# q and k in planes of every fourth token, and DMA transposes from pair 4 on, in an attention and feed-forward kernel

## The chip, the cores and the metric

The kernel runs on one core of one Trainium2 chip. The metric is the time of one execution on the device in microseconds (us), the median of several. Executions of one kernel lie within 1.3% of each other here (the kernel before: 345.49 to 350.08 us). A profile is of one execution and has a span of its own, a little shorter than the time (346.3 us). Engines in the profile: PE is TensorE (matmuls), DVE VectorE, ACT ScalarE, POOL GpSimd, SP SyncE; on this kernel SP issues all DMA transfers, in order.

## The reference

Attention over 8 batches and 8 heads, 576 tokens of 64 features each, followed by a feed-forward layer on all 4608 tokens:

```
q_d, k_d, v_d = mean of 4 neighbouring tokens of q, k, v        # 144 tokens
out_d     = softmax(q_d k_d^T / 8) v_d, each row repeated 4 times
out_local = softmax(q k^T / 8, only where |i - j| < 4) v
x         = (out_d + out_local), heads side by side             # 4608 x 512
h         = x @ w_in                                            # 512 x 2048
result    = (h - tanh(h)) @ w_out                               # 4608 x 512
```

## The kernel before

Two heads are one *pair*; there are 32 pairs, four to a batch. For each pair q and k are loaded, cast to bf16 rows (`qr`), transposed so that features lie on partitions (the way *forward*), multiplied (`local` scores in five bands, `pooled` scores on sums of four tokens), exponentiated, masked, multiplied by v, normalised (`ln`), and transposed again (the way *back*) into `x`, which the code calls `xT`.

The feed-forward part runs on TensorE in 9 *dense blocks* of 512 tokens: 64 matmuls for the first product (mm1), 64 for the second (mm2). Block 0 needs batch 0 (pairs 0 to 3). **Block 1 needs pairs 0 to 7**, because tokens 512 to 1023 reach into batch 1; block 2 needs pair 11, block 3 pair 15, and so on.

The order of all this is fixed when the kernel is built. Each operation is registered with an engine, an estimated duration and the data that it reads and writes; a list scheduler with those estimates (*the planner*) then fixes each engine's order. On the chip every engine goes through its list in order and waits where something is not ready. Dense matmuls have the lowest priority, so they fill what attention leaves free.

```python
# cut: loads, casts of the weights, pooled v
        if p >= T_DMA:                      # T_DMA = 16: forward by DMA from pair 16 on
            op("SP", 700, lambda: nc.sync.dma_start_transpose(
                out=qT[s].rearrange("p i a g -> p (i a) g"),
                in_=qr[s].rearrange("p i a c -> p (i a c)")), ...)
            op("DMA", 1300, None, ...)      # the planner's estimate of the transfer
            for i in range(2):              # then a reorder of q and of k
                op("ACT", 600, lambda i=i: A.copy(...), ...)
        else:                               # TensorE: 6 transposes each for q and k
            for i in range(2):
                op("PE", 260 * cold, tr, reads=[("qr", s, i), "ident"], ...)
                op("ACT", 540, lambda i=i, b16=b16: A.copy(...), ...)
# cut: two additions for the sums of four; then, before pair 16,
# local scores (s1) and last-band-and-pooled scores (s2) are two blocks in bank pair "ts"
            op("PE", 420 * cold, s1, reads=qks, writes=ts, pri=pri)
# cut: exp on ACT, mask on DVE
            op("PE", 380 * cold, s2, reads=qks + [("qkd", s)], writes=ts, pri=pri)
# cut: exp, mask, outputs (PE, bank pair "ox"), reciprocal and ln (DVE, from "ox")
        if p >= X_DMA:                      # X_DMA = 16: back by DMA from pair 16 on
            op("SP", 600, lambda: nc.sync.dma_start_transpose(
                out=lT[s], in_=ln[s].rearrange("p n c -> p (n c)")), ...)
            # cut: join on DVE or POOL writes xT
        else:                               # 7 transposes on TensorE, then join on DVE
            op("PE", 370 * cold, back, reads=[("ln", s)], writes=ox, pri=pri)
# dense: pri=5000
            op("PE", 432, lambda part=part: mm(part),
               reads=[...] + [("x", b, j) for b in bs for j in range(NP)],
               writes=[("hy", slot)], pri=5000)
    M2_FIRST, T_DMA, X_DMA, NEW = 16, 16, 16, 16
```

The softmax here doesn't subtract the row's maximum and nothing guards it: scores larger than these inputs give would overflow.

## Time and profile before

| | before |
|---|---|
| time, median of 4 | 347.8 us |
| span of the profile | 346.3 us |
| first dense matmul | 32.1 us |
| x of pair 7 written | 74.9 us |
| block 1 starts | 76.4 us |
| from there to the end | 269.9 us |

The start of a block is read from the timeline: its first mm1 matmul, after the 64 of the block before it. Parts of the page, with each digit of a row standing for a fortieth of the span (9 is 90% busy or more; PEclk is the granted TensorE clock in tenths):

```profile
span 346.3 us, 6847 instructions
PE 328.0 (95%) x2556; PEld 163.5 (47%) x2556; DVE 223.8 (65%) x362; ACT 224.8 (65%) x382; POOL 169.9 (49%) x210
...
PE   6787989999999999999999999899999999999995
...
PEclk9698999999999999999999999999999999999999
DMA  8999999999999998999999999645231000100021
...
PE 69%; DVE 10%; ACT 9%; issue 3%; DMA 3%; POOL 2%; SPq 1%; ACTq 0%; POOLq 0%; DVEq 0%
```

Now the path of pair 4 and the end of pair 7 in the timeline (start, duration, engine, line, operation, out<-in; in brackets the idle time before it and what ended it):

```profile
33.38 0.82 POOL L416 CAST qr_86<-qkn_71 96x768 bf16<-96x768 f32 x1 [1.12 <-DMA qkn_71<-in_k_dram]
36.15 0.42 PE L442 MATMUL ps_ts<-ident,qr_86 96*128 96x96 bf16 x6
...
39.17 0.39 PE L478 MATMUL ps_ts<-qk_88 64*128 64x120 bf16 x8
...
51.55 1.09 DVE L556 TENSOR_TENSOR ln_106<-ps_ox,r_104 128x896 bf16<-128x896 f32 x1
...
71.80 1.09 DVE L556 TENSOR_TENSOR ln_107<-ps_ox,r_105 128x896 bf16<-128x896 f32 x1
...
74.15 0.74 DVE L599 TENSOR_TENSOR xT_68<-ps_ox,od_109 128x576 bf16<-128x576 bf16 x1
76.41 0.39 PE L619 MATMUL ps_hy_538<-xT_65,w_in_sb 128*128 128x512 bf16 x1
```

Pair 7's `ln` ends at 72.9 us and its x is complete 2.0 us later. Block 1 starts 1.5 us after that. So x of pair 7 arrives just in time, with nothing to spare.

### The profile page before, as it was taken

The numbers are of one execution on the slowest core, as the hardware profiler recorded it, in microseconds if no ns is written. First come the engines' busy times: TensorE is split into PE (matmuls) and PEld (weight loads), VectorE is DVE, ScalarE is ACT, GpSimd is POOL, SyncE is SP. The second block draws the span as 40 slices with busy tenths as digits, with TensorE's granted clock in tenths as the row PEclk, the third lists the DMA queues.
The fourth block names the chain that finished last, engine by engine and source line by source line (L and its number), as shares of the span: only waits on it lengthen the run. The fifth ranks groups of instructions, "written<-read, shape, count | busy, mean of one in ns | idle before, by whom it ended". The sixth has DMA issues, their size and how long they took to land.

```text
span 346.3 us, 6847 instructions
## 1 busy us (share of the span) xinstructions
PE 328.0 (95%) x2556; PEld 163.5 (47%) x2556; DVE 223.8 (65%) x362; ACT 224.8 (65%) x382; POOL 169.9 (49%) x210
## 2 busy tenths in 40 slices
PE   6787989999999999999999999899999999999995
PEld 2353445555555554445444444444454444444442
DVE  5675788558897968778867677679774443343300
ACT  4585886768978768787878778599753434343411
POOL 6553555575467856887777786958500000000000
PEclk9698999999999999999999999999999999999999
DMA  8999999999999998999999999645231000100021
GB/s 192 234 374 300 277 262 263 217 216 287 212 222 234 252 234 174 226 231 235 261 221 207 260 233 246 157 92 93 57 85 60 31 32 30 61 32 31 30 93 61
DMA packets 103407, 60.74 MB, mean 175 GB/s; under 512 B 77774, under 2 KB 94670, under 8 KB 103374
## 3 DMA queue, kind: packets, MB, share of 16 engines
q1 hardware_dynamic: 103374, 60.30, 78.5%
q8 instruction: 20, 0.33, 0.4%
q14 instruction: 13, 0.11, 0.1%
HBM read 42.46 MB, written 9.44 MB: 150 GB/s over the span
## 4 chain that ended last, share of the span: by engine, by line
PE 69%; DVE 10%; ACT 9%; issue 3%; DMA 3%; POOL 2%; SPq 1%; ACTq 0%; POOLq 0%; DVEq 0%
PE ps_hy_540 L646 8%; PE ps_hy_538 L619 8%; PE ps_hy_539 L619 7%; PE ps_hy_541 L646 7%; PE ps_hy_538 L646 7%; PE ps_hy_539 L646 6%; PE ps_hy_540 L619 6%; PE ps_hy_541 L619 6%; PE ps_ox L538 3%; DVE qr_87 L416 2%; PE ps_ts L478 2%; DMA qkn_73<-in_k_dram 2%; PE ps_ox L545 2%; PE ps_ts L442 2%; PE ps_ox L389 2%
## 5 line engine op out<-in xcount | busy, mean ns | idle before, releaser
L619 PEld LDWEIGHTS <-w_in_sb 128*128 128x128 bf16 x576 | 53.3, 98 | 62.1 <-issue 3.9
L646 PEld LDWEIGHTS <-gT_110 128*128 128x128 bf16 x320 | 30.2, 98 | 34.5
L646 PEld LDWEIGHTS <-gT_111 128*128 128x128 bf16 x256 | 24.0, 98 | 27.4
L459 POOL TENSOR_TENSOR half<-qk_88 128x576 f32<-128x576 bf16 x14 | 16.4, 1169 | 25.3 <-ACT qk_88 L448 11.2
L459 POOL TENSOR_TENSOR half<-qk_89 128x576 f32<-128x576 bf16 x16 | 18.7, 1167 | 19.8 <-ACT qk_89 L448 12.2
L646 PE MATMUL ps_hy_539<-w_out_sb,gT_110 128*128 128x512 bf16 x80 | 20.7, 379 | 0.0
L646 PE MATMUL ps_hy_540<-w_out_sb,gT_110 128*128 128x512 bf16 x80 | 20.4, 379 | 0.0
L646 PE MATMUL ps_hy_538<-w_out_sb,gT_110 128*128 128x512 bf16 x80 | 20.4, 379 | 0.0
L646 PE MATMUL ps_hy_541<-w_out_sb,gT_110 128*128 128x512 bf16 x80 | 20.1, 379 | 0.0
L432 ACT COPY qk_89<-qT_91 128x576 bf16<-128x576 bf16 x16 | 18.7, 1193 | 0.0
L432 ACT COPY qk_88<-qT_90 128x576 bf16<-128x576 bf16 x16 | 18.4, 1188 | 0.0
L511 ACT ACTIVATE E_100<-ps_ts 128x960 bf16<-128x960 f32 x16 | 15.6, 977 | 3.8 <-PE ps_ts L478 3.8
L556 DVE TENSOR_TENSOR ln_106<-ps_ox,r_104 128x896 bf16<-128x896 f32 x16 | 17.4, 1090 | 0.5
L646 PE MATMUL ps_hy_540<-w_out_sb,gT_111 128*128 128x512 bf16 x64 | 16.9, 379 | 0.0
L646 PE MATMUL ps_hy_541<-w_out_sb,gT_111 128*128 128x512 bf16 x64 | 16.8, 379 | 0.0
L646 PE MATMUL ps_hy_539<-w_out_sb,gT_111 128*128 128x512 bf16 x64 | 16.6, 379 | 0.0
L646 PE MATMUL ps_hy_538<-w_out_sb,gT_111 128*128 128x512 bf16 x64 | 16.4, 379 | 0.0
L511 ACT ACTIVATE E_101<-ps_ts 128x960 bf16<-128x960 f32 x14 | 13.6, 973 | 3.8 <-PE ps_ts L478 3.6
L514 DVE TENSOR_TENSOR E_101<-E_101,mask 128x960 bf16<-128x960 bf16 x16 | 13.1, 820 | 3.9 <-ACT E_101 L511 3.7
L556 DVE TENSOR_TENSOR ln_107<-ps_ox,r_105 128x896 bf16<-128x896 f32 x14 | 15.3, 1090 | 0.4
L514 DVE TENSOR_TENSOR E_100<-E_100,mask 128x960 bf16<-128x960 bf16 x16 | 13.6, 847 | 2.8 <-ACT E_100 L511 2.8
L619 PE MATMUL ps_hy_538<-xT_65,w_in_sb 128*128 128x512 bf16 x36 | 13.9, 385 | 1.2 <-DVE xT_68 L599 1.2
(263 smaller groups left out, 890.1 us busy)
## 6 DMA issues: line engine op xcount, KB each, us to landing
out_dram<-y_115 SPq DMA_DIRECT2D x12, 256.0 KB, 2.6
out_dram<-y_116 SPq DMA_DIRECT2D x12, 256.0 KB, 2.3
out_dram<-y_117 SPq DMA_DIRECT2D x12, 256.0 KB, 3.0
qkn_71<-in_q_dram SPq DMA_DIRECT2D x8, 288.0 KB, 7.8
qkn_71<-in_k_dram SPq DMA_DIRECT2D x8, 288.0 KB, 5.8
qkn_72<-in_q_dram SPq DMA_DIRECT2D x8, 288.0 KB, 5.1
qkn_72<-in_k_dram SPq DMA_DIRECT2D x8, 288.0 KB, 5.5
qkn_73<-in_q_dram SPq DMA_DIRECT2D x8, 288.0 KB, 6.6
```

The source lines that it names most:

```text
L389: T.matmul(pv[:, 0, :], pick[:, t, :], vw[w][:, :, t, 0:64], start=(t == 0), stop=(t == NT - 1))
L416: P.choice([(eng, ns, lambda dst=dst, srt=srt, fn=fn: fn(out=dst, in_=srt)) for eng, ns, fn in REORDER[p >= NEARLY][i]], reads=[("qkn", sn ...
L432: op("ACT", 600, lambda i=i: A.copy(out=full[:, i].rearrange("p (g a) -> p g a", a=A6), in_=qT[s][:, i].rearrange("p a g -> p g a")), read ...
L442: T.transpose(b16[:, G6 * a:G6 * a + G6], qr[s][:, i, a, :], ident[0:G6, 0:G6])
L459: eng.tensor_tensor(out=half, in0=four[:, :, :, 0:2], in1=four[:, :, :, 2:4], op=ALU.add)
L478: T.matmul(sc[:, c:c + NQ[t]], qk[s][rows, k0:k0 + 128], qk[s][rows, QW * t:QW * t + NQ[t]], start=True, stop=True)
L511: op("ACT", 870, lambda: A.activation(out=e1, in_=ps[:, :, 0:480], func=AF.Exp, scale=SCALE), reads=ts, writes=[("E", s, 0)], pri=pri)
L514: op("DVE", 700, lambda: V.tensor_tensor(out=e1, in0=e1, in1=mask[:, 0:480].unsqueeze(1).to_broadcast([128, 2, 480]), op=ALU.mult), reads= ...
L538: T.matmul(po[:, hh, 65 * t:65 * t + 65], E[s][:, c:c + 128], vw[w][:, 2 * jj + hh, t, :], start=True, stop=True)
L556: op("DVE", 1010, lambda: V.tensor_tensor(out=ln[s].rearrange("p n (h d) -> p h n d", d=D), in0=blocks[:, :, :, 0:64], in1=r[s].unsqueeze( ...
L619: T.matmul(ps_hy[slot], w_in_sb[:, dc, fc * 128:(fc + 1) * 128], xT[dc][:, kb * 512:kb * 512 + 512], start=(dc == 0), stop=(dc == N_DC - 1))
L646: T.matmul(ps_hy[slot], gT[g][:, fc, ts * 128:ts * 128 + 128], w_out_sb[:, fc, :], start=(fc == 0), stop=(fc == N_FF - 1))
```

## The change

Its intent: (1) take the transposes of pairs 4 to 15 off TensorE in both directions; (2) load q and k so that a row holds 4 tokens instead of 6, which gives four planes of every fourth token: sums of four become additions of planes, q is used in plane order and only k has to be reordered (`kt`); (3) pack the last band and the pooled scores of pair p with the local scores of pair p+1 into one block of TensorE work, the former now in the outputs' bank pair "ox" for every pair from 4 on. In pairs 0 to 3 the transposes stay on TensorE and the pooled sums become matmuls with the identity. The planner's estimates change with it (one exp from 870 to 970 ns, one mask from 700 to 800, from pair 5 on 300 ns of slack before score blocks and outputs). The core of the diff:

```diff
-    M2_FIRST, T_DMA, X_DMA, NEW = 16, 16, 16, 16
+    M2_FIRST, NEW, LATE = 16, 16, 300
# ... loads: 96 rows of 6 tokens become three chunks of 96 rows of 4 tokens
-    qkn = fixed("qkn", [G6, 2, 2, A6 * D], FP32, NQKN)
-    qT = fixed("qT", [128, 2, A6, G6], BF16, 2)
+    qkn = fixed("qkn", [R, 3, 2, 4 * D], FP32, NQKN)
+    planes = fixed("planes", [128, 4, 2 * G], BF16, NPL)
+    kt = fixed("kt", [128, 608], BF16, 2)
# ... forward: bring_rows(p)
+        if p < NP:                                   # NP = 4
+            return
+        op("SP", 700, lambda: nc.sync.dma_start_transpose(
+            out=planes[pl].rearrange("p a (c g) -> p (a c) g", g=R),
+            in_=qr[s].rearrange("p a c d -> p (a c d)")), ...)
# ... bring_sums(p): k reordered on DVE, ACT or POOL; planes added on DVE or POOL
# ... one score block
+    def scores(p):
+        def mm():
+            mixed_mm(p, flat2(ps_ox), 72 if p >= NEW else 16)
+            if p + 1 < NPAIR:
+                local_mm(p + 1, flat2(ps_ts), range(4), None)
+        keys = mixed_keys(p) + (local_keys(p + 1) if p + 1 < NPAIR else [])
+        op("PE", 640, mm, reads=keys, writes=["ox"] + [("ts", 0), ("ts", 1)], ...)
# ... back: give_back(p)
-        if p >= X_DMA:
+        if p >= NP:
             op("SP", 600, lambda: nc.sync.dma_start_transpose(
                 out=lT[s], in_=ln[s].rearrange("p n c -> p (n c)")), ...)
```

## The prediction

> **What bounds the kernel now.** By the page, PE is busy 95% of a 346.3 us span and holds 69% of the chain of waits. In the timeline a dense matmul (128x512) issues every 0.216 us; 1152 of them make 249 us. The first starts at 32.1 us; attention is interleaved on PE until 254 us.
>
> A second bound hides before 75 us. In the table of 1 us windows the DMA share is at or above 1.0 in every window from 24 to 66 us: w_in, w_out and q, k, v loads queue behind each other (7 to 12 us from issue to landing). Dense block 1 needs pairs 0 to 7. The last x piece of pair 7 is written at about 74.3 us; block 0 runs out of matmuls at 75.4 us. So PE work there is only just enough: removing some gains nothing unless pair 7 is ready earlier.
>
> **What the change removes.** For pairs 4 to 15, 12 forward transposes (0.51 us of PE) and 7 back transposes (0.50 us) per pair: 12.1 us. One score block in place of two saves a switch gap, about 0.13 us per pair, 1.6 us. From pair 16 on, two ACT reorders from SBUF (1.19 us each) become one on any of three engines; ACT and DVE (65% busy each) are off the critical path there. In pairs 0 to 3 the pooled sums move from DVE/POOL (1.17 + 0.74 us on POOL) to 16 short matmuls: 1 to 2 us at most.
>
> **What it adds.** 24 more DMA transposes. In the DMA windows after 225 us, where little else runs, a transpose fills the engines for about 1.35 us (295 KB: 218 GB/s) and lands about 5 us after issue. The Trainium skill, "DMA: Bandwidth & Descriptors", section "Latency and other measured facts", gives 261 GB/s for a transpose with a non-contiguous middle dimension; this trace is somewhat below. The q/k loads get 1 KB rows: about neutral. The score block of pair p also needs pair p+1's k: pair 7 waits for pair 8.
>
> **Cost on the critical path.** The saturated queue gets about five transposes (7 us) before pair 8 lands; each pair's chain gets two landings of 5 to 6 us in place of PE work. I estimate from these durations that pair 7's x arrives at 80 to 88 us instead of 74, while PE runs dry at 67 to 70 us. So pairs 4 to 7's saving is lost and 5 to 14 us more is paid. From there on about 9 us is saved (pairs 8 to 15); later the attention pace (7 to 8 us per pair by DMA) stays under the 8.2 to 8.6 us that PE needs for a pair plus its share of dense work.
>
> Net: between -8 and +6 us. Prediction 344.5 us (334 to 354). Faster by over 2%: 0.36; within 2%: 0.48; slower by over 2%: 0.16.
>
> **What would show it.** Right: PE idle between about 65 and 85 us, ended by x or scores that waited for DMA; block 1 starting after 76 us; from then on about 264 us instead of 270; DMA share at or above 1 until 150 us or later. Wrong: block 1 starting before 75 us (about 335 us); or PE stalls spread over pairs 16 to 31, behind late transposes in a fixed PE order (above 350 us).
>
> **What would make it wrong.** If the queue has slack that I read as saturation, or transposes get in early, the whole 13 us is gained. If SP, which issues all DMAs in order, blocks on transposes, both stages are late.

## More of the kernel before

TensorE is busy throughout and is 69% of the chain of waits. The same by stages, from the table of windows (window; its length; for PE, PEld, DVE, ACT, POOL the busy time and the count of instructions; clock; DMA share; GB/s):

```profile
60.00:80.00 20.00, 19.97 (x214) 11.33 (x212) 12.01 (x21) 13.98 (x26) 13.27 (x16) 1.00 1.20 223
80.00:100.00 20.00, 19.97 (x212) 11.14 (x210) 18.04 (x30) 17.60 (x35) 10.40 (x13) 1.00 1.18 250
160.00:180.00 20.00, 20.00 (x158) 9.78 (x157) 15.09 (x22) 15.62 (x24) 15.30 (x20) 1.00 1.17 231
180.00:200.00 20.00, 20.00 (x162) 10.02 (x161) 14.22 (x24) 15.95 (x26) 15.32 (x18) 1.00 1.14 234
```

Pair 4's k rows are ready at 34.2 us, transposed on TensorE from 36.2 us and scored at 39.2 us.

## The result

| | before | after |
|---|---|---|
| time, median of 4 runs | 347.8 us | 385.8 us |
| span of the profile | 346.3 us | 385.2 us |
| first dense matmul | 32.1 us | 43.3 us |
| x of pair 7 written | 74.9 us | 110.9 us |
| block 1 starts | 76.4 us | 110.4 us |
| from there to the end | 269.9 us | 274.8 us |
| mean granted TensorE clock | 0.984 | 0.929 |

The ratio is 1.109 (95% interval 1.103 to 1.116): the mean time of one kernel's fast runs over that of the other's of the same rounds, so not quite the ratio of the medians above. The change makes the kernel 11% slower. The arithmetic of the spans says where: 34.0 us are lost before block 1 starts, 4.9 us after (34.0 + 4.9 = 38.9 = 385.2 - 346.3). The page after:

```profile
span 385.2 us, 6661 instructions
PE 331.0 (86%) x2396; PEld 165.5 (43%) x2396; DVE 254.6 (66%) x396; ACT 207.4 (54%) x367; POOL 170.8 (44%) x195
...
PE   6866799843479849998899899998999999999996
...
PEclk9998799955569958999999999999999999999999
DMA  8999999999998999999999999996220100101012
...
PE 46%; DVE 13%; DMA 8%; POOL 5%; issue 3%; ACT 1%; SPq 1%; POOLq 0%; ACTq 0%; DVEq 0%
```

and the same stages in the table of windows:

```profile
60.00:80.00 20.00, 15.64 (x109) 7.22 (x107) 11.10 (x15) 9.24 (x17) 9.98 (x11) 0.96 1.14 256
80.00:100.00 20.00, 9.29 (x102) 6.59 (x103) 16.77 (x24) 9.18 (x17) 8.58 (x9) 0.50 1.07 237
160.00:180.00 20.00, 17.98 (x154) 8.88 (x151) 19.57 (x25) 14.59 (x28) 16.60 (x17) 1.00 1.08 222
180.00:200.00 20.00, 18.32 (x167) 9.40 (x166) 19.48 (x26) 15.11 (x29) 19.94 (x20) 1.00 1.15 201
```

Two things stand out. There is a hole in TensorE's row between 76 and 110 us (9.3 of 20 us busy, at half clock). Later, VectorE is nearly full (19.6 of 20 us, 15.1 before) and TensorE isn't (18.0 instead of 20). The path of pair 4, and the end of pair 7, in the timeline after:

```profile
36.65 0.61 POOL L423 CAST qr<-qkn 96x512 bf16<-96x512 f32 x1 [1.14 <-DMA qkn<-in_k_dram]
...
52.06 2.71 SPq L429 DMA_TRANSPOSE planes<-qr  x1
...
61.87 0.39 PE L509 MATMUL ps_ts<-planes,kt 64*128 64x120 bf16 x8
...
70.13 0.65 DVE L442 COPY kt<-planes 128x576 bf16<-128x576 bf16 x1 [5.78 <-DMA planes<-qr]
...
71.48 0.22 PE L509 MATMUL ps_ox<-planes,kt 64*128 64x96 bf16 x2
...
74.75 1.09 DVE L619 TENSOR_TENSOR ln<-ps_ox,r 128x896 bf16<-128x896 f32 x1
...
84.00 1.38 SPq L645 DMA_TRANSPOSE lT<-ln  x1
...
97.02 1.09 DVE L619 TENSOR_TENSOR ln<-ps_ox,r 128x896 bf16<-128x896 f32 x1
...
104.86 1.27 SPq L645 DMA_TRANSPOSE lT<-ln  x1
...
109.49 1.22 DVE L629 TENSOR_TENSOR xT<-lT 128x480 bf16<-128x480 bf16 x1
...
110.39 1.47 PE L687 MATMUL ps_hy<-xT,w_in_sb 128*128 128x512 bf16 x3
110.51 0.42 DVE L635 TENSOR_TENSOR xT<-lT 128x96 bf16<-128x96 bf16 x1
```

The rows of pair 4 were cast by 37.3 us, but SP issued their transpose at 52.1, 14.8 us later, behind loads in its list. Local scores came at 61.9 us instead of 39.2. Pair 4's pooled scores then came only at 71.5, 9.6 us later: they share a block with the local scores of pair 5, and the reorder of pair 5's k (the copy `kt` at 70.1) had waited for pair 5's transpose. The transpose at 84.0 us is pair 4's way back. For pair 7, `ln` ended at 98.1 us, SP issued the transpose at 104.9, and x was complete at 110.9: 12.8 us for a way back that took 2.0. Block 1 starts with it; its fourth matmul still waits for the last piece.

x of pair 7 is 36.0 us late. That is a sum of three differences: pair 4's `ln` 23.2 us later (52.6 to 75.8), three more pairs at 7.4 us each instead of 6.8 (2.0 us), and the longer way back (10.8 us).

### The profile page after: what moved, and what is told of

It is laid out like the page before. It is cut to its first block, busy times and chain, and to the rows that moved or that the text cites. A ratio compares the mean times of both kernels' runs of the same rounds, so it can differ in the third digit from the quotient of the medians.

```text
span 385.2 us, 6661 instructions
## 1 busy us (share of the span) xinstructions
PE 331.0 (86%) x2396; PEld 165.5 (43%) x2396; DVE 254.6 (66%) x396; ACT 207.4 (54%) x367; POOL 170.8 (44%) x195
## 4 chain that ended last, share of the span: by engine, by line
PE 46%; DVE 13%; DMA 8%; POOL 5%; issue 3%; ACT 1%; SPq 1%; POOLq 0%; ACTq 0%; DVEq 0%
PE ps_hy L687 21%; PE ps_hy L714 20%; DVE gT L698 4%; DMA planes<-qr 3%; DMA lT<-ln 2%; DMA vst<-in_v_dram 2%; DVE E L543 2%; PE ps_ox L601 2%; DVE kt L442 1%; DVE ln L619 1%; DVE qkd L453 1%; PE ps_ox L608 1%; POOL kt L442 1%; DVE E L561 1%; POOL half L448 1%
## 5 line engine op out<-in xcount | busy, mean ns | idle before, releaser
L687 PE MATMUL ps_hy<-xT,w_in_sb 128*128 128x512 bf16 x576 | 145.1, 388 | 4.7 <-DVE xT L635 2.0
L714 PE MATMUL ps_hy<-w_out_sb,gT 128*128 128x512 bf16 x576 | 140.3, 379 | 0.3 <-DVE gT L698 0.3
L698 DVE TENSOR_TENSOR gT<-ps_hy,u 128x512 bf16<-128x512 f32 x144 | 96.0, 684 | 65.5 <-ACT u L695 65.3
L695 ACT ACTIVATE u<-ps_hy 128x512 f32<-128x512 f32 x144 | 83.9, 597 | 92.7 <-PE ps_hy L687 89.8
L714 PEld LDWEIGHTS <-gT 128*128 128x128 bf16 x576 | 55.0, 98 | 65.1 <-issue 1.2
L423 ACT CAST qr<-qkn 96x512 bf16<-96x512 f32 x51 | 29.6, 615 | 17.7 <-issue 10.2
L619 DVE TENSOR_TENSOR ln<-ps_ox,r 128x896 bf16<-128x896 f32 x32 | 34.8, 1088 | 0.8
L543 DVE TENSOR_TENSOR E<-E,mask 128x960 bf16<-128x960 bf16 x32 | 30.6, 956 | 3.7 <-ACT E L540 3.6
L540 ACT ACTIVATE E<-ps_ts 128x960 bf16<-128x960 f32 x32 | 31.1, 972 | 2.2 <-PE ps_ts L509 2.1
L725 ACT COPY y<-ps_hy 128x512 f32<-128x512 f32 x36 | 21.1, 586 | 19.3 <-PE ps_hy L714 18.9
L448 POOL TENSOR_TENSOR half<-planes 128x576 f32<-128x576 bf16 x20 | 28.1, 1404 | 6.3 <-DMA planes<-qr 6.3
L509 PE MATMUL ps_ts<-planes,kt 64*128 64x120 bf16 x264 | 14.8, 234 | 9.7 <-POOL kt L442 4.9
```

Source lines behind the costliest of these rows:

```text
L423: P.choice([(eng, ns, lambda dst=dst, src=src, fn=fn: fn(out=dst, in_=src)) for eng, ns, fn in CAST_QK], reads=[("qkn", sn, n) for n in ke ...
L448: eng.tensor_tensor(out=half, in0=flat[:, 0:4 * G], in1=flat[:, 4 * G:8 * G], op=ALU.add)
L509: T.matmul(sc[:, c:c + n].rearrange("p (a g) -> p a g", a=4), kt[s][rows, QW * t:QW * t + 128], planes[pl][rows, :, 30 * t:30 * t + n // 4 ...
L540: op("ACT", 970, lambda: A.activation(out=e1, in_=ps[:, :, 0:480], func=AF.Exp, scale=SCALE), reads=[(ts, i) for i in range(2)], writes=[( ...
L543: op("DVE", 800, lambda: V.tensor_tensor(out=e1, in0=e1, in1=mask[:, 0:480].unsqueeze(1).to_broadcast([128, 2, 480]), op=ALU.mult), reads= ...
L619: op("DVE", 1090, lambda: V.tensor_tensor(out=ln[s].rearrange("p n (h d) -> p h n d", d=D), in0=blocks[:, :, :, 0:64], in1=r[s].unsqueeze( ...
```

## The experiments

Eighteen kernels were run. Each was run once for time, beside one run of the kernel before on the same chip (347.3 to 349.8 us), and once for its profile; with one core and one timed run the state is unknown. The four runs of the kernel before lie up to 4.6 us apart, so a difference of less than that between two single runs says nothing by itself. Five of the eighteen (e2, e9, e13, e14, e18) leave data out. The planner makes a new list for every kernel; what a new list alone is worth was never measured, and e13 below suggests that it can be 10 us.

Theory A, the first: **all of the loss is the lateness of pair 7's x, caused by the trips of the DMA transposes.** Rivals: the new layout (E), the granted clock (C), the queue of loads (A2 in the later ones), the chain of one pair (G), and others that are named in the expectations.

| run | what | time | x of pair 7 | block 1 | block 1 to end |
|---|---|---|---|---|---|
| before | | 347.8 | 74.9 | 76.4 | 269.9 |
| after | the change | 385.8 | 110.9 | 110.4 | 274.8 |
| e1 | before, both ways by DMA from pair 4 | 376.6 | 103.6 | 103.9 | 271.0 |
| e5 | before, only back from pair 4 | 372.7 | 94.0 | 93.7 | 277.2 |
| e6 | before, only forward from pair 4 | 379.0 | 97.1 | 98.4 | 278.8 |
| e7 | before, both from pair 8 | 373.3 | 73.2 | 74.3 | 297.3 |
| e8 | after, TensorE transposes to pair 15 | 381.9 | 92.2 | 93.0 | 287.2 |
| e15 | e8, score block cut in two | 380.5 | 87.1 | 91.8 | 287.0 |
| e10 | after, casts of w_in later | 385.8 | 108.3 | 108.2 | 275.9 |
| e11 | after, TensorE kept busy | 385.4 | 109.4 | 108.6 | 275.1 |
| e12 | after, score block cut in two | 381.6 | 104.4 | 105.4 | 274.5 |
| e3 | after, transposes issued before loads | 378.3 | 99.7 | 100.6 | 276.0 |
| e4 | after, transposes issued by ScalarE | 420.5 | 109.8 | 110.3 | 308.5 |
| e2 | after, light loads (wrong results) | 377.6 | 100.6 | 100.5 | 275.3 |
| e9 | e2, planner told (wrong results) | 379.7 | 95.3 | 93.2 | 284.4 |
| e13 | before, light loads, planner told (wrong) | 359.1 | 76.0 | 77.3 | 279.9 |
| e14 | e1, light loads, planner told (wrong) | 378.1 | 85.7 | 86.6 | 289.8 |
| e16 | e3, e10 and e12 together | 387.4 | 95.5 | 94.7 | 291.0 |
| e17 | e16, reorder of k on ScalarE | 376.5 | 96.2 | 95.4 | 279.3 |
| e18 | e17, no pooled sums (wrong results) | 372.3 | 95.4 | 94.4 | 276.1 |

All are us; x and block 1 count from the start of the span; the last column is the span minus block 1's start. In e9 to e12, e17 and e18 the trace lacks one or two of block 0's 64 records, and the start is that of the first mm1 matmul after the pause.

### Which part of the change: e1, e8

e1 does one part alone, in the kernel before:

```diff
-    M2_FIRST, T_DMA, X_DMA, NEW = 16, 16, 16, 16
+    M2_FIRST, T_DMA, X_DMA, NEW = 16, 4, 4, 16
```

> The kernel before with one thing changed: both DMA transposes start at pair 4 instead of 16; its layout, adds and two score blocks stay. Queue theory (transposes of pairs 4 to 15 sit behind prefetched loads on one DMA queue, so pairs 4 to 11 are late and PE runs dry): 370 to 390 us, dense block 1 starts after 95 us, granted clock falls below 0.96. Rival, the layout theory (the new layout, the sums from planes and the score block that needs the next pair make the chain long): 345 to 352 us, block 1 at about 75 us.

Measured: 376.6 us. The early DMA transposes alone, without any of the layout, cost 28.6 us of span, and nearly all of it lies before block 1 (27.5 us: 103.9 instead of 76.4; from there on 271.0 instead of 269.9).

e8 does the opposite: the new layout, with the transposes of pairs 4 to 15 back on TensorE by the code that pairs 0 to 3 use.

```diff
-        if p < NP:
+        if p < T_FWD:                  # T_FWD, T_BACK = 16, 16
             return
-        if p >= NP:
+        if p >= T_BACK:
             op("SP", 600, lambda: nc.sync.dma_start_transpose(
```

> The kernel after, with its new layout, new pooling and mixed score block kept, but the transposes of pairs 4 to 15 put back on TensorE, both ways, by the code that pairs 0 to 3 use in it. Theory A (the DMA transposes of the first batches cost, the layout is at most a few us): x of pair 7 comes at 76 to 88 us and the time is 348 to 358 us; the first dense matmul stays near 43 us, because that start belongs to the layout. Rival E (the layout, its mixed score block that ties pair p+1 to pair p, and its later start cost most of the loss): over 368 us.

Measured: 381.9 us: theory A's 348 to 358 is missed, and the rival's figure came. Pairs 4 to 7 follow at 11.3 us (`ln` ends at 55.5, 68.6, 80.9, 89.4 us) instead of 6.8. So the layout is no bystander: in the way that this kernel runs it on TensorE, with the planner's changed estimates, it costs as much as the transposes. Half of e8's loss lies before block 1 (16.6 us) and half after it (17.3). In the change the two don't add up; that each makes the same x late is my reading of it, not shown by a run of its own.

### Which direction, and from which pair: e5, e6, e7

Each changes the same one line of the kernel before: T_DMA, X_DMA = 16, 4 (e5), 4, 16 (e6), 8, 8 (e7).

> The kernel before with one number changed: the transposes BACK (attention output to x) go by DMA from pair 4 on instead of from pair 16 on; the transposes forward stay on TensorE until pair 16. Theory A (all of the loss is the lateness of pair 7's x, because dense block 1 starts the moment it is written): in the trace of the change the way back took 12.8 us (normalised output written 98.1, x written 110.9) against 2.0 before, so x of pair 7 comes at 84 to 88 us instead of 74.9, block 1 starts within 1 us of it, and the time is 355 to 362 us (before 348). Rival B (what costs is the forward way alone, since the back way is off the chain): at most 351 us. Rival C (any early DMA transpose jams the queue of loads for everything): over 368 us.

> The kernel before with one number changed: the transposes FORWARD (q and k rows to planes) go by DMA from pair 4 on; those back stay on TensorE until pair 16. Theory A: with both directions early, pair 4's attention was done at 71.4 us instead of 52.6 (18.8 us later), pair 7's at 92.2 instead of 72.9 (19.3 later), so with the back way on TensorE x of pair 7 comes at about 92 to 96 us and the time is 364 to 371 us, and the two directions add up to the 28 us that both cost together. Rival B (the directions hinder each other in the one queue, so each alone costs little): under 360 us.

> The kernel before with both directions by DMA from pair 8 on, instead of 16 (the run of this with 4 was 376.6). Theory A (it is the first batch with DMA transposes that comes late, and how much of that shows depends on how far x is ahead of its dense block there): block 1 starts on time, 76 to 78 us; x of pair 11 comes 20 to 28 us late (105.2 before), block 2 needs it at 106.5, so the same stall stands one block later, a little shorter: 362 to 372 us. Rival D (it is only the jam of the load queue in the first 66 us, where every 1 us window of the DMA engines is full, so that from pair 8 on transposes are nearly free): 348 to 353 us.

Measured: 372.7, 379.0 and 373.3 us. e5 and e6 miss the ranges: each direction alone costs about what both cost together (24.6 and 30.9 us of span against 28.6), and e5's time lies in the range of rival C (over 368), the jam of the queue that e7 tests next. Of e5's loss 7.4 us and of e6's 8.9 us lie after block 1, so not all of it is pair 7's x. x of pair 7 was 19.1 us late with the back way alone, 22.2 with the forward way alone, 28.7 with both. The back way alone is longer than I had worked out from the change: pair 4's `ln` ended at 50.5 us, SP issued its transpose at 62.75, and x was complete at 72.2. In this stage a transfer that is ready waits for its turn on SP whichever way it goes; that with both ways part of one wait lies within the other is my reading of the sums.

e7 decides between a jam of the first 66 us and a first batch that is always late. Block 1 starts on time, at 74.3 us. Then x of pair 11 comes at 129.0 instead of 105.2, and block 2 starts at 126.5 instead of 106.5: the stall has moved by one block and is 20 us long. The time is 1.3 us over the range of theory A and 20 over rival D's. Rival D falls. With the switch at pair 4 and at pair 8 alike, the cost falls on the first batch with DMA transposes, where x is not ahead of its dense block. The kernel before switches at pair 16, where that lead exists: x of pair 15 is there at 130.9 us and block 3 starts at 142.7.

### What is not the cause: e10, e11, e12

e10 brings the first dense matmul forward, e11 keeps TensorE's clock up, e12 cuts the score block.

```diff
# e10
-    T_QK, T_V, T_W, W_PRI, NEARLY = 700, 900, 2850, -3, NP
+    T_QK, T_V, T_W, W_PRI, NEARLY = 700, 900, 2850, 31, NP
-        pri = 10 * p - 12
+        pri = 10 * p - (12 if p < NP else 0)
# e11, in the emission of TensorE's list between block 0 and block 1
+            if more.get(i):            # into a bank that is free there
+                for _ in range(more[i]):
+                    T.matmul(ps_hy[0], ident, w_in_sb[:, 0, 0:512], start=True, stop=True)
# e12
-        op("PE", 640, mm, reads=keys, writes=["ox"] + [("ts", 0), ("ts", 1)], ...)
+        op("PE", 320, lambda: mixed_mm(p, ...), reads=mixed_keys(p), writes=["ox"], ...)
+        op("PE", 400, lambda: local_mm(p + 1, ...), reads=local_keys(p + 1), ...)
```

> The kernel after, with the casts of w_in (and the row casts of pairs from 4 on) planned behind the exponentials of pairs 2 and 3, so that the first dense matmul comes earlier: 35 to 38 us instead of 43.3. Theory A (dense block 0 has 27.6 us of matmuls and block 1 waits for pair 7's x at 110.9, so the late start lies in the shade of that): block 1 starts at 107 to 112 us and the time stays within 3 us of the change's 385.8. Rival E (the late start adds its 11 us to the end): 374 to 379 us.

> The kernel after with some 60 dummy matmuls of 512 columns, spread before the score and output matmuls in the dry stretch between dense block 0 and dense block 1, so that TensorE is not idle there (the granted clock was 0.50 from 80 to 112 us). They write a bank that nobody reads. Theory A (the half clock is a result of the idling, and only stretches the short matmuls of the chain): granted clock 0.9 or more in 80 to 100 us, x of pair 7 comes 2 to 5 us earlier, 380 to 385 us. Rival C (the half clock makes the stretch long): 375 us or less.

> The kernel after with the mixed score block cut in two again: the pooled scores of pair p no longer wait for pair p+1's k. In the change local scores of pair 4 ran at 61.9 us and its pooled ones at 71.5, after pair 5's transpose. Theory A: pair 4 is done 5 to 9 us earlier, but pairs still follow at 7 us each behind the same transposes, so x of pair 7 comes 3 to 8 us earlier and the time is 377 to 383 us. Rival E (the coupling is the main cost): 368 us or less.

e10: the first dense matmul comes at 39.0 us (not quite the 35 to 38 expected) instead of 43.3, and the time is 385.8 as in the change. What e10 wins back of the late start lies in the shade of the wait for pair 7.

e11: 385.4 us, and x of pair 7 comes 1.5 us earlier (2 to 5 were expected). This window of its table is to be held against the change's own for 80 to 100 us (9.29 us busy, clock 0.50):

```profile
80.00:100.00 20.00, 14.22 (x125) 7.32 (x124) 15.97 (x23) 8.18 (x15) 7.75 (x7) 0.93 1.17 235
```

The clock is back and the time is not. The Trainium skill, "TensorE: Matmul & The Clock Gate", section "Part 1: The HAM clock gate", says that idling lets the clock fall to half; the traces agree (0.50 after the idling began, 0.93 where dummy matmuls fill it). But here the half clock is a symptom. Rival C falls.

e12: 381.6 us. Pair 4's `ln` ends at 67.3 instead of 75.8 us, x of pair 7 comes 6.5 us earlier, and 4 us of time are won, no more than the scatter of the kernel before. The coupling is a part, not the main one.

### The order of issue: e3, e4

```diff
# e3: loads of pair p (from 6 on) are listed after the transpose of pair p - 2
-        op("SP", ns, fn, writes=list(keys) + ["queue", ("q", keys[0])], pri=pri)
+        op("SP", ns, fn, reads=after, writes=list(keys) + ["queue", ("q", keys[0])], pri=pri)
+    def behind(p):
+        return [("plq", (p - 2) % NPL)] if p - 2 >= NP else []
# e4: all transposes go through ScalarE's queue; the planner gives them a lane of their own
-        op("SP", 700, lambda: nc.sync.dma_start_transpose(
+        op("ACT", 700, lambda: nc.scalar.dma_start_transpose(
```

> The changed kernel; the loads of pair p (from 6 on) may not be issued before the transpose of pair p-2 has been issued. Same bytes, same instructions. Queue theory: the first transposes no longer wait behind the loads of pairs 6 and 7, block 1 starts about 7 us earlier (near 103 us), total 372 to 380 us. Bandwidth theory (the added transposes simply need too much DMA time): unchanged within 1%, 382 to 389 us. Layout theory: unchanged.

> The changed kernel with all transposes issued from ScalarE's DMA queue instead of SP's, so that they do not queue behind loads; the order planner is told that they have a lane of their own. Same bytes. Queue theory: block 1 starts 10 to 25 us earlier (85 to 100 us), total 355 to 370 us although ScalarE pays over 1 us for each issue. Bandwidth theory: total unchanged or worse, 383 to 395 us.

e3: 378.3 us, the queue theory's figure; the bandwidth and layout theories, which expected no change, fall. Pair 4's transpose goes out at 42.5 us instead of 52.1 (6.3 us after its rows are ready, at 36.2) and x of pair 7 comes 11.2 us earlier. The way back is not helped: 14.1 us from `ln` to x for pair 7.

e4: 420.5 us, 50 us above its expectation. The first transposes do go out early (37.5 and 45.8 us), but the third only at 60.9. ScalarE too works through its list in order, and now its exponentials and tanh stand in one list with the transposes: in the list of waits ScalarE's casts of q and k wait 29.1 us for transposes that have to read the same row buffer first. Which of its waits is to blame is left open.

### How much is the queue, how much the trip: e2, e9, e13, e14

These take away the bytes in the queue: from pair 5 on q and k bring a sixth of their rows and v a fifth, so the results are wrong.

```diff
-                    out=qkn[s][r0:r0 + rows, c],
+                n = rows if p < 5 else rows // 6
+                    out=qkn[s][r0:r0 + n, c], ...
+                elif p >= 5:
+                    nc.sync.dma_start(out=t[:, i, 1:2], in_=win(QW - 4, 128, 1))
# e9, e13, e14 only: the planner's estimates of these loads too
-            load(450, issue, [("qkn", s, n)], T_QK * rows / R, -30)
+            load(450, issue, [("qkn", s, n)], T_QK * rows / R / (6 if p >= 5 else 1), -30)
```

> The changed kernel, with wrong results on purpose: from pair 5 on (v) and pair 5 on (q, k) each load brings a sixth (q, k) or a fifth (v) of its rows, with the same number of DMA issues in the same order; every other instruction is the same. Queue theory: the backlog ahead of the transposes is gone from 35 us on, block 1 starts before 90 us, total 350 to 365 us. Layout theory, or a theory that SP's issue rate or the bare landing time of a transpose is the limit: at least 378 us, block 1 after 105 us.

> As the light loads run (from pair 5 on the loads bring a sixth of q and k and a fifth of v; results wrong on purpose), but now the kernel's own planner, which fixes each engine's order, is told that these loads are cheap too. In the light loads run TensorE was still busy without a gap until 72 us and met the scores of pair 4 at 69.3 us, where the old order had put them behind some 100 dense matmuls, so that run could not show what an empty queue is worth. Theory A2 (the transposes' trips are long because they stand in a full DMA queue, and the fixed order was built round that): x of pair 7 comes at 80 to 88 us, block 1 starts with it, and the time is 352 to 362 us. Rival G (the chain of one pair is long by itself: trip, reorder, scores, exp, mask, output, trip): x of pair 7 at 95 us or later, the time 370 us or more.

> Control: the kernel before, transposes where it has them (DMA from pair 16), with the light loads of the ninth run (a sixth of q and k, a fifth of v from pair 5 on, planner told so; results wrong on purpose). Both theories: TensorE bounds it, so little changes, 338 to 350 us, x of pair 7 at 66 to 77 us.

> The kernel before with DMA transposes both ways from pair 4 on (376.6 us with full loads, x of pair 7 at 103.6), now with the light loads and the planner told so. In the new layout the same step took x of pair 7 from 110.9 only to 95.3. Theory A2 (in the old layout the wait in the DMA queue is nearly all of the delay): x of pair 7 at 77 to 84 us, 348 to 358 us. Rival G (a pair's chain with two trips is long without any queue): x of pair 7 at 90 us or later, over 364 us.

e2 gave 377.6 us, but it was not a clean test. TensorE was busy without a gap until 72 us, and the scores of pair 4 stood at 69.3 us in its list behind more than 100 dense matmuls, because the planner still believed in heavy loads. **A run that makes something earlier shows little when the order of the engine that would profit is fixed for it to be late.** e9 tells the planner. e13 is the control, and it missed its range: the kernel before became 10 us slower with light loads, nearly all of it after block 1 starts (279.9 us instead of 269.9). I put that down to the list that the planner makes for them; it was not tested. So the times of these runs can't be compared with the others, but their first stage can, against the control's x of pair 7 at 76.0 us:

- Old layout: 28.7 us late with full loads (e1), 9.7 us late with light ones (e14, 85.7). Both theories had named a side; it is in between, nearer to A2. By this difference about 19 us are owed to the full queue and about 10 us remain. These are not the bare trips: from its rows being ready to its issue pair 4's transpose waited 20.4 us in e1 and still 9.6 us in e14, behind other entries of SP's list.
- New layout: 36.0 us late with full loads, 19.3 with light ones (e9, 95.3): about 17 us of queue, and 19 of chain, some 10 more than in the old layout. Here too the wait for issue is part of the rest (14.8 us in the change, 10.6 in e9). Rival G's figure came for e9. In e9 x of pair 3 is 9.8 us later than in the control (41.2 against 31.4), which is as much as that difference; whether it is the cause was not tested by itself.

These shares are differences between runs whose lists differ, so they are rough.

### Do the repairs add up? e15 to e18

e15 is e8 with e12's cut. e16 is the change with e3's, e10's and e12's edits together. e17 is e16 with the reorder of k on ScalarE, e18 is e17 without the two additions for the pooled sums (wrong).

```diff
# e17
-    REORDER = [("DVE", 800, V.tensor_copy), ("ACT", 1200, A.copy),
-               ("POOL", 1100, GP.tensor_copy)]
+    REORDER = [("ACT", 1200, A.copy)]
# e18, besides
-        P.choice([... add1 ...], reads=[("pl", pl)], writes=["half"], pri=pri)
-        P.choice([... add2 ...], reads=["half"], writes=[("qkd", s)], pri=pri)
```

> The new layout with TensorE transposes until pair 16 (381.9 us; its pairs followed each other at 11.3 us from pair 4 to 7, against 6.8 before), now with the mixed score block cut in two. Theory E1 (the coupling makes this slow: pair p's pooled scores wait for pair p+1's transposes, which wait for the one score bank): pairs at most 9 us apart, x of pair 7 at 80 to 88 us, 364 to 374 us. Rival E2 (twelve transposes, sixteen pooling matmuls, three copies and the scores through the one bank are slow by themselves): still over 10 us apart, 376 us or more.

> The kernel after with the three repairs that were tried singly: loads issued behind the transposes (alone 378.3), score block cut (381.6), casts of w_in later (385.8). Theory A and G: the chain of two trips stays, x of pair 7 at 88 to 96 us, 368 to 375 us. Rival (what they cost was mostly the queue order and the coupling, and they hide each other): under 362 us.

> The three repairs together (387.4 us, span 385.7), with the reorder of k from the planes put on ScalarE for every pair, where before has its reorder; the choice among VectorE, ScalarE and GpSimd is taken away. There, from 120 to 280 us, VectorE was busy 17.4 of 20 us (14.5 in before), and its operations with both inputs in SBUF were stretched: joins of 128x480 took 3.1 us on average instead of the 1.2 that one takes undisturbed, masks of 128x960 1.0 instead of 0.63. Theory H (from pair 8 on attention is paced by VectorE, stretched by GpSimd's work on SBUF, so that what the repairs won is lost again): VectorE busy at most 16.8 of 20 in that stage, dense blocks 2 to 7 closer together, 374 to 382 us. Rival I (the serial chain of one pair through the output bank paces it, whoever does the reorder): 385 to 390 us.

> As e17, and the two additions that make the pooled q and k are left out from pair 4 on (the pooled scores then use what pair 2 or 3 left; results wrong on purpose), which takes about 1.9 us a pair from GpSimd or 1.5 from VectorE. Theory H: VectorE busy at most 15.8 of 20 us from 120 to 280 us, 364 to 376 us. Rival I: 383 us or more.

e15: 380.5 us, rival E2's figure, though x of pair 7 (87.1) is in theory E1's range. The pairs follow at 9.5 us (`ln` 55.4 to 84.0 us in three steps), between what the two sides had said. So why the new layout is slow with TensorE transposes is not settled.

e16: 387.4 us, outside both expectations, though x of pair 7 (95.5) is where theories A and G had it. Block 1 starts at 94.7 us, 15.7 earlier than in the change, and then all of it is given back: from there to the end 291.0 us instead of 274.8. Each of blocks 2 to 4 starts within 4 us of the writing of its last x (block 2 at 126.2, x of pair 11 at 127.7; block 3 at 166.0, 165.3; block 4 at 204.4, 208.1): attention now paces these blocks, at 8 to 11 us a pair. The reason that I tested is that VectorE's operations are stretched. Here is one mask of e16 in the timeline:

```profile
173.10 1.16 POOL L445 COPY kt<-planes 128x576 bf16<-128x576 bf16 x1
173.22 2.79 DVE L546 TENSOR_TENSOR E<-E,mask 128x960 bf16<-128x960 bf16 x1
174.21 1.28 POOL L451 TENSOR_TENSOR half<-planes 128x576 f32<-128x576 bf16 x1
```

The mask, about 0.65 us when undisturbed, took 2.79 us, over two operations of GpSimd, and ended half a microsecond after the second. The Trainium skill, "SBUF — State Buffer", section "Who interferes with whom", says that VectorE and GpSimd share a pair of SBUF ports and that a VectorE instruction with two SBUF inputs contends with a GpSimd instruction that reads SBUF, while one with at most one SBUF input outside the two-port modes does not. The traces agree. In e16 the 14 masks of this shape during which GpSimd ran nothing took at most 0.66 us and the other 18 took 1.07 on average; the joins (two of 16 undisturbed) took 1.23 and 2.37; `gT`, with one input in PSUM, took 0.69 either way. From 120 to 280 us, grouped by shape (count, then busy us and mean ns), first the kernel before, where the names carry buffer numbers, so that a row holds only one buffer's operations:

```profile
L514 DVE TENSOR_TENSOR E_100<-E_100,mask 128x960 bf16<-128x960 bf16 x8 | 7.6, 956 | 2.1 <-ACT E_100 L511 2.0
L514 DVE TENSOR_TENSOR E_101<-E_101,mask 128x960 bf16<-128x960 bf16 x8 | 6.9, 857 | 2.9 <-ACT E_101 L511 2.8
L582 DVE TENSOR_TENSOR xT_67<-lT_102 128x480 bf16<-128x480 bf16 x2 | 1.4, 697 | 0.0
```

the kernel after:

```profile
L698 DVE TENSOR_TENSOR gT<-ps_hy,u 128x512 bf16<-128x512 f32 x71 | 47.3, 679 | 7.0 <-ACT u L695 7.0
L543 DVE TENSOR_TENSOR E<-E,mask 128x960 bf16<-128x960 bf16 x21 | 23.4, 1114 | 0.4 <-ACT E L540 0.3
L442 DVE COPY kt<-planes 128x576 bf16<-128x576 bf16 x9 | 14.2, 1577 | 0.0
...
L629 DVE TENSOR_TENSOR xT<-lT 128x480 bf16<-128x480 bf16 x6 | 8.0, 1334 | 5.9 <-DMA lT<-ln 5.9
```

e16:

```profile
L630 DVE TENSOR_TENSOR xT<-lT 128x480 bf16<-128x480 bf16 x8 | 25.8, 3221 | 1.6 <-DMA lT<-ln 1.6
L546 DVE TENSOR_TENSOR E<-E,mask 128x960 bf16<-128x960 bf16 x17 | 17.6, 1035 | 1.8 <-ACT E L543 1.8
```

and e17:

```profile
L546 DVE TENSOR_TENSOR E<-E,mask 128x960 bf16<-128x960 bf16 x19 | 16.6, 873 | 4.1 <-ACT E L543 3.9
L630 DVE TENSOR_TENSOR xT<-lT 128x480 bf16<-128x480 bf16 x9 | 13.7, 1526 | 4.0 <-DMA lT<-ln 4.0
```

The subtraction `gT` keeps its 0.68 us; the masks, the joins and the copy `kt`, all in SBUF, are stretched, the joins of e16 to 3.2 us. (`kt` has a single input, which the two-input rule doesn't cover; whether it ran in a two-port mode the traces don't say.) The masks are stretched in the kernel before as well; what the change adds is the copy `kt` and longer joins. The new joins are also longer to begin with (1.22 us undisturbed against 0.65), presumably because they write every fourth element; that was not tested.

e17 takes one operation off the pair of engines: 376.5 us, as theory H had it, 11 us less than e16, with VectorE busy 16.6 of 20 us from 120 to 280 us instead of 17.4. e18 takes two more: 372.3 us, 4.2 us less, which is within the scatter. Rival I, that whoever does the reorder doesn't matter, had expected 385 us or more for e17 and falls; theory H had named both times. What is not excluded is that the new lists have a share in the 11 us. And in e18 VectorE is busy only 13.7 of 20 us, less than in the kernel before (14.5), and from block 1 on it still takes 276.1 us against 269.9: VectorE is not all of it either, and the rest stays open. No version beat the kernel before.

## Why the prediction was wrong

**What bounds the kernel: right.** Block 1 waits for pair 7's x, with nothing to spare. e1, e5 and e6, in the old layout, all start block 1 within 1.3 us of it, and so does the change.

**"pair 7's x arrives at 80 to 88 us": the step that failed.** It came at 110.9. The term was "two landings of 5 to 6 us" and "five transposes (7 us) before pair 8 lands". That counted how long the transposes occupy the DMA engines and how long one takes from issue to landing, and took issue itself as immediate. What was left out is the time from data being ready to issue: 14.8 us forward for pair 4, 6.8 us back for pair 7, because SP goes through one list in order, with loads ahead of the transposes. The fullness of the queue is only part of it: of the 14.8 us, 10.6 remain with light loads (e9) and 6.3 with the transposes listed ahead of later loads (e3). With the landing and the join the way back was 12.8 us. Two more terms were too small for pair 4: its landing forward took 8.4 us (issue at 52.1, the first operation that waited for it at 60.5), and the coupling, for which the prediction gave no time, held its pooled scores back by 9.6 us behind pair 5's transpose; without the coupling (e12) x of pair 7 came 6.5 us earlier. The light loads put about 17 of the 36 us down to the queue. The Trainium skill, "VectorE: DVE Perf Modes", section "The three transpose paths", gives 390 ns on TensorE against 1309 ns by DMA for 128x128 in bf16, a difference of 0.9 us; no run here times such a transpose by itself. That is the price of an operation, and here the way back alone became 10.8 us longer. The prediction named this, as what would make it wrong ("If SP, which issues all DMAs in order, blocks on transposes, both stages are late"), and gave it no number.

**Pairs 0 to 3, "1 to 2 us at most": wrong, and as far as tested without effect.** The first dense matmul came 11.2 us later. e10 undid 4.3 us of that and the time did not move; the other 6.9 us were not tested.

**"From there on about 9 us is saved": the sign was wrong.** From block 1 on the change needs 4.9 us more, not some 6 to 9 us less. The transposes did leave TensorE (2396 matmuls instead of 2556), but nothing came of the room: blocks 2 and 3 started 34 to 36 us late, like block 1 (140.8 instead of 106.5, 178.3 instead of 142.7), and block 4 40 us late (216.9 instead of 176.9), although its last x had been there since 200.8. From 160 to 217 us the list of waits gives TensorE 5.1 us of waiting, all of it ended by VectorE. And VectorE, which I had called off the critical path at 65%, was a stage average: it is at 19.5 of 20 us between 160 and 200 us, since the new joins, the reorder and the additions were placed on it and on GpSimd, whose work stretches it. The 65% and the 66% after it hide that.

**"PE idle between about 65 and 85 us": right in kind, too short.** It began at about 76 us and lasted until block 1: TensorE was busy 13.6 of 34 us between 76 and 110 us. Of the tells of "wrong" that I had listed, the spread of stalls over pairs 16 to 31 is seen only weakly; the main stall is the one that I had listed as right ("block 1 starting after 76 us"), only far longer.

**Theory A, after the result, was too simple as well.** x of pair 7 explains e1 (28.7 us late, 28.6 lost) and where 34 of the change's 38.9 us lie. It does not explain the times of e8, e14 or e16, where x of pair 7 was earlier again and the time was not. Behind the first limit stood a second one.

## What to carry to other kernels

Moving work from a full engine to an idle path helps only if the consumer can wait: cost the whole trip, from ready through the issuing engine's list and the queue to the join, at the point where the result has the least lead, and move the work where the lead exists (here pair 16, not pair 4 or 8). When several small repairs each give a little, run them together before believing their sum; a second limit may stand right behind the first. And an experiment that makes data early is only a test if the fixed order of the consumer lets it use them.

## What the Trainium skill lacked or had wrong

- "DMA: Bandwidth & Descriptors" has bandwidths, a first-byte latency and the cost of descriptors. I found in it no figure for what a transfer waits before its issue on an engine that issues in order: here 14.8 us (pair 4 forward), 6.8 us (pair 7 back), 12.2 us (pair 4 back in e5). The issue of one transpose also occupied SP for 1.3 us in the median of the light-load runs before 120 us and for up to 5.5 us with full loads (5.46 in the change, the second of them).
- "VectorE: DVE Perf Modes", "The three transpose paths", compares durations of one transpose only (390 and 1309 ns). In a chain with a consumer that waits, the way back was 2.0 us on TensorE and 12.8 us by DMA.
- "TensorE: Matmul & The Clock Gate", in its list of terms, estimates the penalty of throttling as the throttled time times (1 - K/N). From 80 to 112 us the clock was 0.50, which would make 16 us by that; lifting it to 0.95 (e11, the same window) changed the time by 0.3 us, within the scatter. In this stage TensorE was not the limit, and the estimate did not hold.
- "SBUF — State Buffer", "Who interferes with whom", is confirmed in its rule (VectorE with two SBUF inputs is stretched, about 0.65 to 2.79 us for a mask; with one input in PSUM it keeps 0.68 us). It has no example of what a mix of both engines' work costs in a kernel: here moving one 128x576 copy a pair to ScalarE, with the list that the planner then made, was worth 11 us of 387 (e17 against e16).
